# Linear attention in front of two dense layers: numerators and denominators by token from one product, division on the way out of PSUM, quotients transposed back

## Chip, core and metric

One of the eight cores of a Trainium2 chip runs the whole program in one launch. The metric is device time in microseconds (us) of one execution; lower is better. Beside it stands the span, from the first to the last instruction in the profile of one execution.

## What is computed

Attention by random features, for 4 batches, 8 heads, 576 tokens and 64 columns a head, and then two dense layers on its output, which is laid out as 2304 tokens by 512 columns. All inputs are float32.

```python
def phi(x):
    proj = np.einsum('bhsd,md->bhsm', x, omega)
    sq = np.sum(x * x, axis=-1, keepdims=True) / 2.0
    h = proj - sq
    h = h - np.max(h, axis=-1, keepdims=True)
    return np.exp(h) / np.sqrt(m)
q_p, k_p = (phi(q_s), phi(k_s))
kv = np.einsum('bhsm,bhsd->bhmd', k_p, v)
z = np.sum(k_p, axis=2)
num = np.einsum('bhsm,bhmd->bhsd', q_p, kv)
den = np.einsum('bhsm,bhm->bhs', q_p, z)[..., None] + 1e-06
x = num / den                       # then [2304, 512]
x = leaky_relu(x @ w_in, 0.01) @ w_out
h = x @ w_in2
out = (h * clip(h + 3, 0, 6) / 6) @ w_out2
```

There are 128 features (m), so a tile of features of 128 tokens is a square of 128 by 128.

## The kernel before

The program is written as a graph of operations. Each names its engine (or several, with a planned cost for each), what it reads and writes, and a due time; `Graph.run` then plays the program through with those costs and puts every engine's instructions into a fixed order. TensorE's order is therefore decided when the kernel is built, and a matmul that is not ready holds up everything behind it.

**Groups.** The 2304 tokens are cut into five groups of 512, 256, 512, 512 and 512 (`GN`). Group 0 has its attention done first; then the first dense layer (`moe1`) of group 0 runs on TensorE, with the attention of group 1 sprinkled between its matmuls, and so on up to group 4 (the `att` stage, about 47 to 357 us). The second dense layer (`moe2`) of all groups is last, from about 519 us. The dense layers hold each float32 number as two fp32r halves and make a product of three matmuls (lines 497 to 499 in `mm3`, 1067 and 1167).

**Pairs of heads.** The two heads of a pair (e = 0, 1) lie on 64 partitions each. `scores` (L744, with tails of 64 tokens in `K_tail`, L765) multiplies 64 rows of a head by omega, DVE takes the minimum of a row (L709), adds and subtracts squares (L712, POOL L715), and ACT makes the exponentials (L720): the features `h`, one bank for each head, tokens on the partitions.

**K_unit(b, hp)**, 16 of them, 4 in the attention of each of groups 0 to 3 (batch 0 to 3), makes what all queries of a pair of heads need. For batches 0 and 1 (`OLDKV` = 2) `kv` (L791) multiplies features by values, nine matmuls: `v` has a column of ones behind each head's 64, so that column 64 of the result `kvf` (features by 66 columns a head) is z. One copy on ACT (L795) brings it to SBUF, and two matmuls (`rep`, L802) spread z over all partitions as `zr`, which is copied on (L478). For batches 2 and 3 `kvt` (L813) makes the product the other way round, 64 columns of the array for each head, ten matmuls; a copy, a transpose (L820) and a copy give `kvf`, and z is made apart: DVE sums the features over the tiles (L830) or POOL does (L828), POOL adds the tail (L835), and a matmul by ones (L839) sums over the partitions into `zr`.

**Q_first**, four units of group 0, transposes the features (L858), multiplies by all 66 columns of `kvf` (L867), so that numerators and the denominator of a token lie in one row, adds epsilon, takes the reciprocal and multiplies on DVE while reading PSUM (L872, L874, L876), and transposes the quotients back (L885).

**Q_unit** does the queries of groups 1 to 4 in 17 units, each of up to four tiles a head: `f` full tiles of 128 tokens for each of `nh` pairs of heads, and with `half` a tile that holds 64 tokens of both heads. By `f` times `nh` and half tiles: five units have four full tiles, four have three full tiles, four have three full and one half tile, two have two and two, and two have four half tiles alone (17 in all, of which the list `PARTS` gives the tokens). In each, DVE makes the denominators before anything else: for every tile a product of features and `zr` summed along the row (L915, with an instruction that reads the sum), then a reciprocal (L921). POOL or DVE scales the features by it (L926). TensorE transposes the scaled features (L941), they are copied to `tq`, and `num` (L972) multiplies 64 columns of `kvf` by them, for each head, straight into the layout that `moe1` reads (columns on the partitions, tokens along the row).

**PSUM and SBUF.** In the `att` stage attention may hold four of the eight banks at a time (`held` and `share` in `Graph.run`). `keep_warm` (L1364) puts matmuls on zeros where the player of the order expects TensorE to idle in the first stage.

Of the kernel before, what the change touches and what calls it, by code (L numbers as in the profile page):

```python
# [14 lines left out]
ALU = mybir.AluOpType  # L15
# [28 lines left out]
OLDKV = 2  # L44
# [307 lines left out]
def attn_moe_kernel(ctx: ExitStack, tc: tile.TileContext, qT, kT, qn, kn, v1, om2, w1i, w1o, w2i, w2o, out):  # L352
# [23 lines left out]
    def duo(t, later=0):  # L376
# [17 lines left out]
        "junk": many(1, "junk", ([128, 2, 128], BF16), pool=misc),  # L394
# [6 lines left out]
        "zr": many(6, "zr", ([128, 2, 128],), pool=right),  # L401
# [4 lines left out]
        "hh": many(2, "hh", ([128, 128],), pool=right),  # L406
        "ht": many(2, "ht", ([128, 512],), pool=right),
        "tq": many(1, "tq", ([128, 2, 512],), pool=right),
# [56 lines left out]
    ones = sb("ones", [128, 128])  # L465
    zero = sb("zero", [128, 128], F32R)
    slots["den"] = many(3, "den", ([128, 4, 1],), ([128, 4, 1],))
# [256 lines left out]
    def scores(f, half, xsrc, nsrc, due, nh=1):  # L724
# [9 lines left out]
        hs = [Buf("h" if c > 1 else "hh") for c in cols]  # L734
# [36 lines left out]
    kvf, zrep = {}, {}  # L771

    def K_unit(b, hp, due):
        v = Buf("v")
        hs, _ = scores(4, False, kT[b, hp, :, 0:512], kn[b, hp, :, 0:8], due)
        ht = last64[b]
        g.op(dma(lambda: v.tiles[0][:, 0:5 * 132], v1[b, hp], 128 * 5 * 132 * 4), wr=[v], due=due - 7e3)
        zr = zrep[b, hp] = Buf("zr")
        kf = kvf[b, hp] = Buf("kvf")
        p = Ps(g.use)  # L780


        if b < OLDKV:
            def kv():
                todo = [(slice(0, 132), ht.tiles[0][:, hp * 128:hp * 128 + 128], v.tiles[0][:, 4 * 132:5 * 132])]
                for i in range(4):
                    for e in range(2):
                        w = slice(e * 66, e * 66 + 66)
                        todo.append((w, hs[e].tiles[0][:, i * 128:i * 128 + 128], v.tiles[0][:, i * 132 + w.start:i * 132 + w.stop]))
                for n, (w, l, r) in enumerate(todo):  # L790
                    nc.tensor.matmul(p.tiles[0][:, w], lhsT=l, rhs=r, start=n == 0, stop=n == len(todo) - 1, skip_group_check=True)  # L791

            g.op([("pe", 9 * 215.0, kv)], rd=hs + [ht, v], wr=[p], also=[zr, kf], due=due + 3e3)
            kvp = lambda: p.tiles[0][:, 0:132].rearrange("p (h c) -> p h c", h=2)
            g.op([("act", c_act(132, True), lambda: nc.scalar.copy(kf.tiles[0], kvp()))], rd=[p], wr=[kf], due=due + 3e3)  # L795

            flat = lambda: zr.tiles[0].rearrange("p h m -> p (h m)")
            pz = Ps(g.use)

            def rep():  # L800
                for e in range(2):
                    nc.tensor.matmul(pz.tiles[0][:, e * 128:e * 128 + 128], lhsT=kf.tiles[0][:, e, 64:65].to_broadcast([128, 128]),  # L802
                                     rhs=ident, start=True, stop=True)

            g.op([("pe", 360.0, rep)], rd=[(kf, "z")], wr=[pz], due=due + 3.5e3)
            g.op(copy_alts(flat, lambda: pz.tiles[0][:, 0:256], 256, True), rd=[pz], wr=[zr], due=due + 4e3)
            return

        def kvt():
            for i in range(5):  # L810
                for e in range(2):
                    r = ht.tiles[0][:, hp * 128:hp * 128 + 128] if i == 4 else hs[e].tiles[0][:, i * 128:i * 128 + 128]
                    nc.tensor.matmul(p.tiles[0][64 * e:64 * e + 64, 0:128], lhsT=v.tiles[0][:, i * 132 + e * 66:i * 132 + e * 66 + 64], rhs=r,  # L813
                                     start=i == 0, stop=i == 4)

        g.op([("pe", 5 * 224.0, kvt)], rd=hs + [ht, v], wr=[p], also=[zr, kf], due=due + 3e3, mode="N")
        mid = lambda: kf.tiles[0].rearrange("p h c -> p (h c)")[:, 0:128]
        g.op(copy_alts(mid, lambda: p.tiles[0][:, 0:128], 128, True), rd=[p], wr=[kf], due=due + 3e3)
        pt = Ps(g.use)
        g.op([("pe", 112.0, lambda: nc.tensor.transpose(pt.tiles[0][:, 0:128], mid(), ident))], rd=[kf], wr=[pt], due=due + 3e3)  # L820
        g.op(copy_alts(lambda: kf.tiles[0][:, :, 0:64], lambda: pt.tiles[0][:, 0:128].rearrange("p (h c) -> p h c", h=2), 128, True),
             rd=[pt], wr=[kf], due=due + 3.5e3)
        for e in range(2):
            H, Z = lambda e=e, i=0: hs[e].tiles[0][:, i * 128:i * 128 + 128], lambda e=e: zr.tiles[0][:, e]

            def adds(e=e, H=H, Z=Z):
                for i in range(3):
                    nc.gpsimd.tensor_tensor(out=Z(), in0=Z() if i else H(), in1=H(i=i + 1), op=ALU.add)  # L828

            g.op([("dve", c_dve(512), lambda e=e, Z=Z: nc.vector.tensor_reduce(  # L830
                out=Z(), in_=hs[e].tiles[0].rearrange("p (q f) -> p f q", q=4), axis=AX.X, op=ALU.add)),
                ("pool", 3 * c_pool(128), adds)], rd=[hs[e]], wr=[(zr, e)], due=due + 3e3)
            R = lambda e=e: (zr.tiles[0][64 * e:64 * e + 64, e], ht.tiles[0][64 * e:64 * e + 64, hp * 128:hp * 128 + 128])
            g.op([("dve", c_dve(128), lambda R=R: nc.vector.tensor_tensor(out=R()[0], in0=R()[0], in1=R()[1], op=ALU.add), True),
                  ("pool", c_pool(128), lambda R=R: nc.gpsimd.tensor_tensor(out=R()[0], in0=R()[0], in1=R()[1], op=ALU.add))],  # L835
                 rd=[ht], wr=[(zr, e)], due=due + 3e3)
        flat = lambda: zr.tiles[0].rearrange("p h m -> p (h m)")
        pz = Ps(g.use)
        g.op([("pe", 435.0, lambda: nc.tensor.matmul(pz.tiles[0][:, 0:256], lhsT=ones, rhs=flat(), start=True, stop=True))],  # L839
             rd=[zr], wr=[pz], due=due + 3.5e3)  # L840
        g.op(copy_alts(flat, lambda: pz.tiles[0][:, 0:256], 256, True), rd=[pz], wr=[zr], due=due + 4e3)
# [5 lines left out]
    def Q_first(b, hp, due):  # L847
# [14 lines left out]
        for e in range(2):  # L862
            p, den = Ps(g.use), Buf("den")

            def num(e=e, p=p):
# [7 lines left out]
                out=den.tiles[0], in0=view()[:, :, 64:65], scalar1=M * EPS, scalar2=None, op0=ALU.add))], rd=[p], wr=[den], due=due + 6e3)  # L873
            g.op([("dve", 90, lambda den=den: nc.vector.reciprocal(out=den.tiles[1], in_=den.tiles[0]), True)], wr=[den], due=due + 6e3)  # L874
            to = lambda e=e: h.tiles[0].rearrange("p (q e c) -> p q e c", q=4, e=2)[:, :, e]
            g.op([("dve", c_dve(256), lambda view=view, den=den, to=to: nc.vector.tensor_tensor(  # L876
                out=to(), in0=view()[:, :, 0:64], in1=den.tiles[1].to_broadcast([128, 4, 64]), op=ALU.mult))],
# [14 lines left out]
    def Q_unit(grp, b, hps, f, half, s0, col0, o, due):  # L892
# [9 lines left out]
        zr, kf = [zrep[b, hp] for hp in hps], [kvf[b, hp] for hp in hps]  # L902
        tq = Buf("tq")
        wide = N > 256
        ts = [Ps(g.use) for _ in range(2 if wide else 1)]
        todo = []
# [46 lines left out]
        elif f:  # L953
            g.op(copy_alts(lambda: tq.tiles[0][:, :, 0:N], lambda: ts[0].tiles[0].rearrange("p (e n) -> p e n", e=2)[:, :, 0:N], 2 * N, True),
                 rd=[ts[0]], wr=[(tq, 0)], due=due + 5e3)
# [483 lines left out]
```

## Time and profile before

| | us |
|---|---|
| median of three timed runs | 880.21 |
| lowest and highest of them | 878.3, 880.41 |
| the profiled execution's own time | 877.54 |
| its span | 875.7 |
| PE (matmul) busy | 860.1, 98% of the span |
| DVE busy | 651.5, 74% |
| ACT busy | 526.4, 60% |
| POOL busy | 176.5, 20% |

The profile shows one execution. PE is TensorE's matmuls and PEld its loads of weights (the stationary operand), which can lie beside matmuls. A matmul's end is modelled and the next starts before it, so that the time a matmul takes of the stream is read from one start to the next, and busy time counts a run's last tail as well. A float32 (not fp32r) matmul shows as two records, each with its own load of weights; a transpose and an fp32r matmul show as one.

### The profile page before, as it was taken

What the parts mean: (1) busy time and instruction counts of PE and PEld (TensorE: products, weight loads), DVE (VectorE), ACT (ScalarE), POOL (GpSimd) and SP (SyncE); (2) the same over time, 40 slices, a digit from 0 to 9 for tenths busy, and PEclk for the clock granted to TensorE, in tenths of its full rate; (3) what the DMA queues carried; (4) which work ended last, traced back from release to release, by engine and by line L of the source; (5) the groups of instructions that cost most, each with busy time, mean ns of one, the idle gap of its engine ahead of it and who ended that gap; (6) DMA issues with size and microseconds to landing.
All of it is one profiled execution on the core that took longest, in us unless ns stands there. A gap on an engine that the chain in (4) does not pass through costs nothing.

```text
span 875.7 us, 17773 instructions
## 1 busy us (share of the span) xinstructions
PE 860.1 (98%) x6340; PEld 782.0 (89%) x6340; DVE 651.5 (74%) x1641; ACT 526.4 (60%) x1196; POOL 176.5 (20%) x300
## 2 busy tenths in 40 slices
PE   9999999999999999999999999999999999999998
PEld 8878788889777878888888888999999999999998
DVE  6997997977987854566688445787678779877765
ACT  7999987877787755544545345544453455445442
POOL 1132212433334322101110001111102203121200
PEclk9999999999999999999999999999999999999999
DMA  9567656887567720798998448885887685688342
GB/s 332 173 196 244 208 175 200 240 250 232 173 174 223 230 97 12 270 359 335 332 350 330 161 140 281 308 300 170 277 300 247 215 271 164 211 264 258 124 147 71
DMA packets 91496, 198.00 MB, mean 226 GB/s; under 512 B 14736, under 2 KB 40976, under 8 KB 91408
## 3 DMA queue, kind: packets, MB, share of 16 engines
q1 hardware_dynamic: 91408, 196.87, 67.9%
q8 instruction: 50, 0.82, 0.4%
q14 instruction: 38, 0.31, 0.1%
HBM read 150.18 MB, written 46.66 MB: 225 GB/s over the span
## 4 chain that ended last, share of the span: by engine, by line
PE 73%; DVE 9%; ACT 8%; DMA 6%; issue 2%; POOL 1%; SPq 1%; DVEq 0%; ACTq 0%; POOLq 0%
PE bank L1067 18%; PE bank L1167 16%; PE bank L497 11%; PE bank L499 11%; PE bank L498 10%; PE bank L744 2%; DMA late_w<-in 2%; DVE junk L915 1%; ACT h L720 1%; DVE nm L709 1%; DMA out_raw<-wt 1%; DMA in_raw<-wt 1%; DVE wst L537 1%; ACT wt L531 1%; ACT wst L527 1%
## 5 line engine op out<-in xcount | busy, mean ns | idle before, releaser
L1067 PE MATMUL bank<-w,g 128*128 128x256 f32 x720 | 95.9, 275 | 0.5 <-ACT bank L1200 0.3
L478 ACT COPY late_u<-bank 128x256 f32<-128x256 f32 (+1 forms) x103 | 39.9, 388 | 85.6 <-PE bank L1167 76.4
L1067 PEld LDWEIGHTS bank<-w,g 128*128 128x128 f32 x720 | 87.9, 192 | 1.0 <-ACT bank L1200 0.4
L1009 DVE TENSOR_TENSOR g<-bank,g 128x512 fp32r<-128x512 f32 (+1 forms) x80 | 50.6, 633 | 38.9 <-ACT g L478 37.8
L720 ACT ACTIVATE h<-bank,nm 128x128 f32<-128x128 f32 x228 | 64.6, 388 | 17.0 <-POOL nm L715 16.8
L1007 ACT ACTIVATE bank<-bank 128x512 f32<-128x512 f32 (+1 forms) x80 | 44.5, 556 | 49.6 <-PE bank L499 49.5
L497 PE MATMUL bank<-x,w 128*128 128x512 f32 (+1 forms) x180 | 67.1, 373 | 0.6 <-DVE g L1009 0.6
L1167 PE MATMUL bank<-x,late_w 128*128 128x256 f32 x528 | 66.9, 276 | 0.1
L497 PE MATMUL bank<-g,w 128*128 128x512 f32 (+1 forms) x180 | 67.0, 372 | 0.1
L499 PE MATMUL bank<-x,w 128*128 128x512 f32 (+1 forms) x180 | 64.6, 359 | 0.9 <-DVE x L481 0.9
L1167 PE MATMUL bank<-second_w,late_w 128*128 128x256 f32 x474 | 64.7, 275 | 0.8 <-ACT late_u L478 0.5
L499 PE MATMUL bank<-g,w 128*128 128x512 f32 (+1 forms) x180 | 64.6, 359 | 0.5 <-DVE g L1009 0.5
L498 PE MATMUL bank<-x,w 128*128 128x512 f32 (+1 forms) x180 | 64.5, 358 | 0.0
L498 PE MATMUL bank<-g,w 128*128 128x512 f32 (+1 forms) x180 | 64.5, 358 | 0.0
L1167 PEld LDWEIGHTS bank<-x,late_w 128*128 128x128 f32 x528 | 62.8, 192 | 0.5 <-DVE late_xr L485 0.3
L709 DVE TENSOR_REDUCE nm<-bank 128x4 f32<-128x512 f32 (+2 forms) x76 | 47.9, 654 | 20.0 <-PE bank L744 19.7
L1167 PEld LDWEIGHTS bank<-second_w,late_w 128*128 128x128 f32 x474 | 58.9, 192 | 1.4 <-ACT late_u L478 0.7
L478 ACT COPY u<-bank 128x256 f32<-128x256 f32 (+1 forms) x52 | 21.9, 426 | 43.7 <-PE bank L1167 22.2
L715 POOL TENSOR_TENSOR nm<-nm,sq 128x4 f32<-128x4 f32 (+2 forms) x76 | 23.0, 311 | 113.7 <-DVE nm L712 106.8
L915 DVE CUSTOM_DVE_ANT_0 junk<-h,zr 128x128 bf16<-128x128 f32 (+1 forms) x128 | 44.1, 381 | 1.3 <-ACT h L720 0.6
L497 PE MATMUL bank<-x,second_w 128*128 128x512 f32 (+1 forms) x120 | 44.1, 368 | 0.8 <-ACT tq L478 0.8
L926 POOL TENSOR_TENSOR h<-h,den 128x512 f32<-128x512 f32 (+2 forms) x32 | 34.0, 1065 | 53.4 <-DVE den L921 42.3
(377 smaller groups left out, 2395.9 us busy)
## 6 DMA issues: line engine op xcount, KB each, us to landing
late_w<-in SPq DMA_DIRECT2D x85, 512.0 KB, 4.5
in<-late_w SPq DMA_DIRECT2D x32, 512.0 KB, 4.4
late_w<-in SPq DMA_DIRECT2D x39, 256.0 KB, 4.8
third_w<-in SPq DMA_DIRECT2D x19, 512.0 KB, 4.8
wst<-w2i SPq DMA_DIRECT2D x16, 512.0 KB, 4.2
wst<-w2o SPq DMA_DIRECT2D x16, 512.0 KB, 4.6
x_t<-late_w SPq DMA_DIRECT2D x12, 512.0 KB, 5.5
v<-v SPq DMA_DIRECT2D x14, 330.0 KB, 4.8
```

The lines of the kernel that those rows point to most:

```text
L478: return [("act", c_act(n, psum), lambda: nc.scalar.copy(dst(), src())), dve if psum else dve + (True,)]
L497: nc.tensor.matmul(o, lhsT=ah, rhs=bh, start=start, stop=False)
L498: nc.tensor.matmul(o, lhsT=al, rhs=bh, start=False, stop=False)
L499: nc.tensor.matmul(o, lhsT=ah, rhs=bl, start=False, stop=stop)
L709: g.op([("dve", c_dve(c * 128), lambda raw=raw, n_=n_: nc.vector.tensor_reduce(out=n_()[:, :, 0], in_=raw(), axis=AX.X, op=ALU.min))], rd= ...
L720: nc.scalar.activation(h.tiles[0][:, q * 128:q * 128 + 128], raw()[:, q], AF.Exp, bias=nm.tiles[0][:, q], scale=-1.0)
L915: nc.vector.tensor_tensor_reduce(out=jk.tiles[0][r, q % 2], in0=h.tiles[0][r, q * 128:q * 128 + 128], in1=zr[k].tiles[0][r, e], scale=1.0, ...
L926: eng.tensor_tensor(out=x, in0=x, in1=den.tiles[1][:, 0:c].to_broadcast([128, c, 128]), op=ALU.mult)
L1007: g.op([("act", c_act(n, True), lambda: nc.scalar.activation(P(), P(), AF.Prelu, alpha=0.01))], wr=[p], due=d)
L1009: g.op([("dve", c_dve(n), lambda: nc.vector.tensor_tensor(out=G1(), in0=P(), in1=G0().bitcast(F32), op=ALU.subtract))], rd=[p, (gg, 0)], w ...
L1067: nc.tensor.matmul(acc[bank].tiles[0][:, half * 256:half * 256 + 256], lhsT=src.tiles[x][:, q * 128:q * 128 + 128], rhs=woven(w[k].tiles[y ...
L1167: nc.tensor.matmul(R[r](), lhsT=w[x], rhs=m[y], start=start and k == n == 0, stop=k == 1 and n == 2, skip_group_check=True)
```

## The change

`Q_unit` of groups 1 to 4 is rebuilt after the pattern of `Q_first`. The scaling ahead of the transposes, the denominators on DVE (L915, L921, L926) and `num` (L972) go. The unscaled features are transposed by bank and copied to `tq`. A new function `quotient` multiplies `tq` by 66 columns of `kvf` for each full tile, or by all 132 for a half tile (whose rows hold 64 tokens of each head), adds epsilon and takes the reciprocal, and divides while reading PSUM into `qt`; for half tiles the reciprocals are first multiplied by a mask `own`, which keeps a row's own head. `back` transposes `qt` to where `num` wrote, and a half tile goes through a matmul with `fold` (two identities of 64 rows, one above the other) instead.

In `K_unit` every batch uses `kv`, without `rep`: `zr`, `kvt`, the transpose, the sums on DVE and POOL and the matmul by ones go. Its planned cost is 220 + 8 times 112 ns where it was 9 times 215; `num`'s in `quotient` is 112 ns a matmul. Buffers: `zr`, `hh`, `ones` and `junk` go, a second `tq`, one `qt`, `fold` and `own` come, `den` has 8 columns. The start gains one DVE addition (`fold`) and three small memsets.

```diff
         "kvf": many(6, "kvf", ([128, 2, 66],), pool=right),
-        "zr": many(6, "zr", ([128, 2, 128],), pool=right),
...
-        "tq": many(1, "tq", ([128, 2, 512],), pool=right),
+        "tq": many(2, "tq", ([128, 2, 512],), pool=right),
+        "qt": many(1, "qt", ([128, 512],), pool=right),
...
-        if b < OLDKV:
-            def kv():
...
-            g.op([("pe", 9 * 215.0, kv)], rd=hs + [ht, v], wr=[p], also=[zr, kf], due=due + 3e3)
...
-            g.op([("pe", 360.0, rep)], rd=[(kf, "z")], wr=[pz], due=due + 3.5e3)
...
-        g.op([("pe", 5 * 224.0, kvt)], rd=hs + [ht, v], wr=[p], also=[zr, kf], due=due + 3e3, mode="N")
...
-        g.op([("pe", 435.0, lambda: nc.tensor.matmul(pz.tiles[0][:, 0:256], lhsT=ones, rhs=flat(), start=True, stop=True))],
...
+        g.op([("pe", 220.0 + 8 * 112.0, kv)], rd=hs + [ht, v], wr=[p], also=[kf], due=due + 3e3)
+        kvp = lambda: p.tiles[0][:, 0:132].rearrange("p (h c) -> p h c", h=2)
+        g.op(copy_alts(lambda: kf.tiles[0], kvp, 132, True), rd=[p], wr=[kf], due=due + 3e3)
...
-                        nc.vector.tensor_tensor_reduce(out=jk.tiles[0][r, q % 2], in0=h.tiles[0][r, q * 128:q * 128 + 128],
-                                                       in1=zr[k].tiles[0][r, e], scale=1.0, scalar=M * EPS, op0=ALU.mult,
-                                                       op1=ALU.add, accum_out=den.tiles[0][r, q])
...
+            def num():
+                at = 0
+                for e, q, m in todo:
+                    w = 132 if m[1] is None else 66
+                    r = kf[m[0]].tiles[0].rearrange("p h c -> p (h c)") if m[1] is None else kf[m[0]].tiles[0][:, m[1]]
+                    nc.tensor.matmul(p.tiles[0][:, at:at + w], lhsT=tq.tiles[0][:, e, q * 128:q * 128 + 128], rhs=r, start=True, stop=True)
+                    at += w
...
+            g.op([("dve", 75, lambda: nc.vector.tensor_scalar(out=dd(0), in0=V()[:, :, :, 64:65], scalar1=M * EPS, scalar2=None, op0=ALU.add))],
+                 rd=[p], wr=[den], due=due + 6e3)
...
+            g.op([("dve", c_dve(tiles * 64), lambda: nc.vector.tensor_tensor(
+                out=to(), in0=V()[:, :, :, 0:64], in1=dd(1).to_broadcast([128, dd(1).shape[1], dd(1).shape[2], 64]), op=ALU.mult))],
+                rd=[p, den], wr=[(qt, sub)], due=due + 6e3)
...
-                    nc.tensor.matmul(p.tiles[0][64 * e:64 * e + 64, k * n:k * n + n], lhsT=kf[k].tiles[0][:, e, 0:64],
-                                     rhs=tq.tiles[0][:, e, k * n:k * n + n], start=True, stop=True)
...
+                for i in range(f):
+                    c = (k * f + i) * 128
+                    nc.tensor.transpose(p.tiles[0][:, k * n + i * 128:k * n + i * 128 + 128], qt.tiles[0][:, c:c + 128], ident)
+                if half:
+                    c = (T + k) * 128
+                    nc.tensor.matmul(p.tiles[0][:, k * n + F:k * n + n], lhsT=qt.tiles[0][:, c:c + 128], rhs=fold, start=True, stop=True)
```

In the changed kernel the lines move: `mm3` is 495 to 497, `scores` 742, `kv` 787, the transposes of the features 860, `num` 875, the division 881 to 889, `back` 921 and 924, `keep_warm` 1318. Counted over the whole program, TensorE has 72 `kv` matmuls more (144 for 72), 96 `num` matmuls of 66 columns and 16 of 132, 48 transposes and 16 folds in `back`, and 44 matmuls on zeros for 36.

The first place is the batch-2 K_unit on PE. Before: ten matmuls of 64 array columns (`h`, `ht` features, `v` values), and behind other work the transpose of `kvf` and the matmul by `ones`.

```order
L499 MATMUL bank_177<-x_104,w_95 128x256
L813 MATMUL bank_182<-h_0_149,v_0_144 64x128
L813 MATMUL bank_182<-h_0_145,v_0_144 64x128
...
L813 MATMUL bank_182<-ht_0_152,v_0_144 64x128 x2
L497 MATMUL bank_180<-g_105,w_94 128x256
...
L820 MATMUL bank_181<-ident,kvf_0_130 128x128
...
L839 MATMUL bank_178<-zr_0_136,ones 128x256
```

The changed kernel, the same unit:

```order
L921 MATMUL bank_176<-ident,qt_0_147 128x128 x3
L787 MATMUL bank_170<-v_0_137,ht_0_143 128x132
L787 MATMUL bank_170<-v_0_137,h_0_139 128x66
L787 MATMUL bank_170<-v_0_137,h_0_140 128x66
...
L787 MATMUL bank_170<-v_0_137,h_0_140 128x66
L495 MATMUL bank_175<-g_106,w_90 128x256
```

Nine matmuls of 128 array columns stand there in one run, and nothing of the unit comes later on PE.

The second place is a query unit of group 4 (one pair of heads, four full tiles) on PE. Before: both banks of features (`h`) are transposed together, and `num` follows 15 dense matmuls later.

```order
L941 MATMUL bank_177<-ident,h_0_145 128x128 x4
L941 MATMUL bank_176<-ident,h_0_147 128x128 x4
L497 MATMUL bank_180<-g_106,second_w_5_0_1039 128x512
...
L499 MATMUL bank_178<-x_102,second_w_8_0_1042 128x512
L972 MATMUL bank_182<-tq_0_154,kvf_0_130 64x512 x2
L497 MATMUL bank_178<-x_103,second_w_8_0_1042 128x512
```

The changed kernel:

```order
L860 MATMUL bank_176<-ident,h_0_142 128x128 x4
...
L860 MATMUL bank_173<-ident,h_0_139 128x128 x4
L875 MATMUL bank_169<-kvf_0_129,tq_0_146 128x66 x4
L495 MATMUL bank_170<-x_103,second_w_6_0_1012 128x512
...
L875 MATMUL bank_176<-kvf_0_129,tq_0_146 128x66 x4
L495 MATMUL bank_171<-g_106,second_w_5_0_1011 128x512
...
L497 MATMUL bank_173<-x_102,second_w_8_0_1014 128x512
L921 MATMUL bank_169<-ident,qt_0_147 128x128 x4
L495 MATMUL bank_173<-x_103,second_w_8_0_1014 128x512
```

Two wide matmuls have become eight narrow ones in two runs, 9 dense matmuls apart, and four transposes come 15 dense matmuls after the second.

## Rows read from the trace of the kernel before

**Rows 1.** The page: span, and busy time by engine.

```profile
span 875.7 us, 17773 instructions
...
PE 860.1 (98%) x6340; PEld 782.0 (89%) x6340; DVE 651.5 (74%) x1641; ACT 526.4 (60%) x1196; POOL 176.5 (20%) x300
...
PEclk9999999999999999999999999999999999999999
```

**Rows 2.** The page: the chain that ended last, by engine.

```profile
PE 73%; DVE 9%; ACT 8%; DMA 6%; issue 2%; POOL 1%; SPq 1%; DVEq 0%; ACTq 0%; POOLq 0%
```

**Rows 3.** Waits of PE: who waited for whom, us in total, times, longest.

```profile
PE bank L499 <- DVE g L1009: 1.3, 2, 0.8
PE bank L1364 <- POOL zero L1355: 1.1, 1, 1.1
PE bank L499 <- DVE x L481: 0.9, 1, 0.9
PE bank L885 <- DVE u L876: 0.8, 1, 0.8
...
PE bank L497 <- DVE g L1009: 0.6, 1, 0.6
```

**Rows 4.** Timeline of PE: start, us, instruction; a kv run between dense matmuls.

```profile
115.03 0.38 PE L499 MATMUL bank<-x,second_w 128*128 128x512 f32 x1
115.25 0.39 PE L791 MATMUL bank<-v,ht 128*128 128x132 f32 x2
115.47 1.90 PE L791 MATMUL bank<-v,h 128*128 128x66 f32 x16
...
117.47 0.38 PE L498 MATMUL bank<-x,second_w 128*128 128x512 f32 x1
```

**Rows 5.** Timeline of PE: a query unit's num, then transposes, between dense matmuls.

```profile
316.55 0.38 PE L499 MATMUL bank<-g,w 128*128 128x512 f32 x1
316.86 1.08 PE L972 MATMUL bank<-tq,kvf 128*64 128x512 f32 x4
...
318.19 0.38 PE L498 MATMUL bank<-x,second_w 128*128 128x512 f32 x1
318.40 0.38 PE L499 MATMUL bank<-x,second_w 128*128 128x512 f32 x1
318.62 1.04 PE L941 MATMUL bank<-ident,h 128*128 128x128 f32 x8
...
319.71 0.38 PE L498 MATMUL bank<-x,second_w 128*128 128x512 f32 x1
```

**Rows 6.** Timeline of PE: a kvt run of batch 2 between dense matmuls.

```profile
187.48 0.28 PE L498 MATMUL bank<-x,w 128*128 128x256 f32 x1
187.60 0.28 PE L499 MATMUL bank<-x,w 128*128 128x256 f32 x1
187.80 1.09 PE L813 MATMUL bank<-h,v 128*64 128x128 f32 x16
...
189.26 0.28 PE L498 MATMUL bank<-g,w 128*128 128x256 f32 x1
```

**Rows 7.** Groups by line on PE: busy us, mean ns; idle before, releasers.

```profile
L972 PE MATMUL bank<-tq,kvf 128*64 128x64 f32 (+5 forms) x112 | 15.9, 395 | 0.0
L1364 PE MATMUL bank<-zero 128*128 128x384 f32 x36 | 10.1, 432 | 1.1 <-POOL zero L1355 1.1
L802 PE MATMUL bank<-ident,kvf 128*128 128x128 f32 x32 | 5.3, 288 | 0.7 <-ACT kvf L795 0.7
L839 PE MATMUL bank<-zr,ones 128*128 128x256 f32 x16 | 5.2, 408 | 1.1 <-ACT h L720 0.6 <-POOL zr L835 0.5
```

**Rows 8.** Groups by line on DVE and POOL, same columns.

```profile
L915 DVE CUSTOM_DVE_ANT_0 junk<-h,zr 128x128 bf16<-128x128 f32 (+1 forms) x128 | 44.1, 381 | 1.3 <-ACT h L720 0.6
L876 DVE TENSOR_TENSOR u<-bank,den 128x256 f32<-128x256 f32 x8 | 3.3, 416 | 0.0
L874 DVE RECIPROCAL den<-den 128x4 f32<-128x4 f32 x8 | 1.4, 169 | 0.0
L872 DVE TENSOR_SCALAR den<-bank 128x4 f32<-128x4 f32 x8 | 1.2, 155 | 0.3 <-ACT zr L478 0.2
L926 POOL TENSOR_TENSOR h<-h,den 128x512 f32<-128x512 f32 (+2 forms) x32 | 34.0, 1065 | 53.4 <-DVE den L921 42.3 <-DVE nm L712 3.3 <-ACT wst L527 2.4
```

More of the change, by code (lines that the diff above doesn't have):

```diff
@@ L464, in attn_moe_kernel @@
     wn = sb("wn", [128, 128])
[L465 removed]
     zero = sb("zero", [128, 128], F32R)
[L467 removed]
+    slots["den"] = many(3, "den", ([128, 8, 1],), ([128, 8, 1],))
+    fold = sb("fold", [128, 64])
+    own = sb("own", [128, 2, 1])
     three = sb("three", [128, 8], pool=misc)[:, 0:1]
@@ L733, in scores @@
         ps = [Ps(g.use) for _ in cols]
-        hs = [Buf("h" if c > 1 else "hh") for c in cols]
+        hs = [Buf("h") for c in cols]
         def mm():
@@ L823, in K_unit @@
[L823 to L836, printed above, removed]
@@ L956, in Q_unit, with tr @@
-        if half:
-            from_ = lambda: ts[1 if wide else 0].tiles[0][:, nh * F:nh * F + nh * 128].rearrange("p (h e n) -> p e h n", h=nh, e=2)
-            g.op(copy_alts(lambda: T()[:, :, :, F:n], from_, nh * 128, True), rd=[ts[1 if wide else 0]], wr=[(tq, 2)], due=due + 5e3)
+        kf, tq, qt = [kvf[b, hp] for hp in hps], Buf("tq"), Buf("qt")
+        T = nh * f
+        for bank, (h, c) in enumerate(zip(hs, cols)):
+            ts = Ps(g.use)
+            def tr(h=h, ts=ts, c=c):
+                for q in range(c):
+                    x = slice(q * 128, q * 128 + 128)
+                    nc.tensor.transpose(ts.tiles[0][:, x], h.tiles[0][:, x], ident)
+            g.op([("pe", c * 109.0, tr)], rd=[h], wr=[ts], also=[tq], due=due + 5e3)
+            g.op(copy_alts(lambda bank=bank, c=c: tq.tiles[0][:, bank, 0:c * 128], lambda ts=ts, c=c: ts.tiles[0][:, 0:c * 128], c * 128, True),
+                 rd=[ts], wr=[(tq, bank)], due=due + 5e3)
@@ new lines, in Q_unit @@
+        full = lambda: qt.tiles[0][:, 0:T * 128].rearrange("p (t e c) -> p e t c", e=2, c=64)
+        for es in ([0, 1],) if T <= 3 else ([0], [1]):
+            if T:
+                w = len(es) * T * 66
+                todo = [(e, (k * (f + half) if e == 0 else k * f) + i, (k, e)) for e in es for k in range(nh) for i in range(f)]
+                quotient(todo, [(tq, e) for e in es], len(es) * T, len(todo) * 112.0,
+                         lambda t, w=w, es=es: t[:, 0:w].rearrange("p (e t c) -> p e t c", e=len(es), c=66),
+                         lambda es=es: full()[:, es[0]:es[-1] + 1], False, es[0])
@@ L959, in Q_unit @@
+        for k0 in range(0, nh if half else 0, 2):
+            ks = range(k0, min(nh, k0 + 2))
+            c = T * 128 + k0 * 128
+            quotient([(0, k * (f + half) + f, (k, None)) for k in ks], [(tq, 0)], 2 * len(ks), len(ks) * 224.0,
+                     lambda t, m=len(ks): t[:, 0:m * 132].rearrange("p (k e c) -> p k e c", k=m, c=66),
+                     lambda c=c, m=len(ks): qt.tiles[0][:, c:c + m * 128].rearrange("p (k e c) -> p k e c", k=m, c=64), True, 2 + k0)
         away = grp == NG - 1
@@ L1356, in attn_moe_kernel @@
         make_identity(nc, ident)
+        nc.vector.tensor_tensor(out=fold, in0=ident[:, 0:64], in1=ident[:, 64:128], op=ALU.add)
+        nc.vector.memset(own, 0.0)
+        nc.vector.memset(own[0:64, 0], 1.0)
+        nc.vector.memset(own[64:128, 1], 1.0)
         nc.vector.tensor_scalar(out=wn, in0=wn, scalar1=-scale, scalar2=None, op0=ALU.mult)
```

115 lines of the change are left out of this document (26 added, 89 removed).

## The prediction

> **What bounds the kernel now.** I read the page's busy times first: PE is busy for 860.1 of a span of 875.7 us, DVE for 651.5, POOL for 176.5, and the clock row is at 9 in every slice, so TensorE runs at its upper level of 2.4 GHz throughout [rows 1]. The chain that ended last is PE for 73% of the span [rows 2]. What PE does not fill is 875.7 - 860.1 = 15.6 us, and that is the most that any relief of another engine can bring. The waits of PE show where part of it lies: dense matmuls that wait for DVE's low half of their operands (L499 and L497 for g L1009, 1.3 and 0.6 us, and L499 for x L481, 0.9), a transpose in Q_first that waits 0.8 us for its quotient (L885), and 1.1 us at the start [rows 3]. The groups by line add 0.7 us ahead of L802 and 1.1 ahead of L839 [rows 7]. So the question is how much TensorE time the change adds, for nearly all of it lies on the path.
>
> **The price of a matmul on PE.** It is read from starts, not from durations. Dense matmuls of 512 columns start 0.216 us apart (318.19 to 318.40, the last digit rounded) [rows 5], those of 256 columns 0.112 (187.48 to 187.60) [rows 6]. A run of something else between two of them costs the time from the last dense start before to the second dense start behind it, less two dense steps; the second, because the first one behind a run is itself held up.
>
> - kv, nine float32 matmuls and thus 18 records: 117.47 - 115.03 = 2.44, less 0.43, is 2.01 us, or 0.112 a record and 0.224 a matmul [rows 4]. Eight of the nine have 66 columns, so this is the price of a matmul of 66 columns.
> - num for 512 tokens: 318.19 - 316.55 = 1.64, less 0.43, is 1.21 us, where its busy time is 1.08; the run pays 0.12 or so beyond its busy time, on the way into and out of half the array's columns [rows 5].
> - eight transposes: 319.71 - 318.40 = 1.31, less 0.43, is 0.88, or 0.110 each [rows 5].
> - kvt: 189.26 - 187.60 = 1.66, less two steps of 0.112, is 1.44 us [rows 6].
>
> The program plans a 66-column matmul at 112 ns, half of what the row shows. The Trainium skill says under "FP8 and Floating Point Precision", section TensorE Precision Notes, that a true float32 product takes four passes through the array. By it alone, 66 columns four times are 264 columns, at 2.4 GHz an estimated 110 ns, which is the planned price and would make this change cheap. The row does not agree: kv takes 0.224, the pace of its two loads of weights rather than of its columns, and the sum below goes by the row.
>
> **What goes from PE.** num in 17 units: 15.9 us busy [rows 7] and 17 times 0.12, 17.9. kvt in 8 units, 8 times 1.44 = 11.5. Behind each a transpose at 0.110, 0.9, and the matmul by ones: its two records are busy for 5.2 / 8 = 0.65 us, of which a part overlaps what follows [rows 7]; two steps of a 512-column record, 0.43, are my value, so 3.5 in all (it could be 5.2). The spreading of z in the 8 other units is four records at 0.112, 0.45, so 3.6 (busy 5.3 at most [rows 7]). Together 37.4 us, up to 40.8 with the two upper ends.
>
> **What comes to PE.** Eight more kv runs at 2.01, 16.1. In quotient 96 matmuls of 66 columns and 16 of 132, all at 0.224 (the kv run holds one of 132 and is no dearer), 25.1. In back 48 transposes at 0.110, 5.3. The 16 folds have 64 columns, a form that the trace doesn't show: at least a transpose, 0.110, at most a kv matmul, 0.224; they are float32 products with 128 rows of weights, as kv is, so 0.224, 3.6 (1.8 at the least). Together 50.1. The transposes of the features stay the same number. The eight more matmuls on zeros cost nothing if PE would have idled there and 10.1 / 36 = 0.28 each at most, 2.2 us [rows 7]; I take half, 1.1. PE gains 50.1 + 1.1 - 37.4 = 13.8 us of work, between 7.5 (folds cheap, zeros free, the removed ones at their busy time) and 15.
>
> **What leaves the other engines.** DVE loses the 44.1 us of L915, POOL the 34.0 us of L926 [rows 8]. DVE gains 30 quotients of 0.155 + 0.169 + 0.416 = 0.74 us, 22 us, priced by the same three instructions of Q_first [rows 8]. This is worth nothing in itself, because both lie beside PE; it is worth what PE waited for them. The waits ahead of L802 and L839 go with these instructions, 0.7 + 1.1 = 1.8 us [rows 7]. The three dense waits for DVE, 1.3 + 0.9 + 0.6 = 2.8 [rows 3], should go too, because DVE no longer has runs of L915 of 381 ns apiece between PE and the low half that PE waits for. That is 4.6 us back. It can be nothing, or the whole 15.6 less the 1.1 of the start, 14.5.
>
> **The waits that the change adds.** A quotient waits for its num, and back waits for both quotients with all dense matmuls of the next rows queued behind it. In the query unit of group 4 shown above, 15 dense matmuls at 0.216, 3.2 us, stand between the second num and back, while DVE needs 0.74 and the signals, which leaves room for other work ahead of it in DVE's queue. The cover is long enough there. num waits for the copy of tq, which has 9 dense matmuls of cover and the other head's run for either head. A second tq lets the next unit begin before the last is through. At the start, fold and three memsets go onto DVE while the first scores wait for their input, and cost nothing. SP gets no further transfers. I price new waits at zero.
>
> **The sum.** 13.8 - 4.6 = 9.2 us longer. The profiled execution had 877.54 us and its span with 1.8 us around it; so 886.7 for such an execution. The median of the runs is 880.21, 2.7 above the profiled one, and the forecast is for a median: 880.2 + 9.2 gives 889.4, rounded to **890 us**. About 0.3% is what a measurement of this kernel can tell from no change, 2.6 us to either side of 880.2.
>
> **Rivals.**
>
> - *The division becomes a wait on PE.* Unlike the scaling by POOL, the quotient stands between two matmul steps of the same unit. If back, in all 17 units, waited as L885 did in Q_first, 0.8 us [rows 3], that were 13.6 us, and no relief elsewhere: 880.2 + 13.8 + 13.6 = 908. For it: Q_first has this very pattern and does wait. Against: there PE has little else to put between, here it has 3.2 us of dense matmuls. It decides once DVE takes over 3 us from num to the last product. Half of it gives 898. Chance 0.13.
> - *All waits go.* DVE and POOL are so much lighter that PE hardly idles any more: 880.2 + 13.8 - 14.5 = 879.5, within 0.3%. For it: DVE at 74% is the engine behind most of the waits that rows name. Against: those waits add up to a third of the 15.6, and the rest also lies in the second layer and at the start, where nothing changes. It needs more than 11 us of the 15.6. Chance 0.08.
> - *The planned price holds, and the kernel becomes faster.* If a 66-column matmul in quotient and kv ran at the pace of its columns, at 0.112, the 64 new ones in kv and 96 in quotient would be 160 times 0.112 = 17.9 us cheaper: 13.8 - 17.9 - 4.6 = -8.7, or 871.5 us. The skill's rule of four passes, named above, speaks for it. Against it stand the rows of kv in this very form [rows 4], and nothing in the new product lets two loads of weights overlap. The point is 0.14 us a matmul: below it the added work is less than the waits won. Chance 0.05. That the change would not do what it says isn't among the rivals, since the order of instructions shows the new matmuls.
>
> **How the numbers follow.** The forecast with its own bounds (work 7.5 to 15, relief 0 to 7) has 0.74 and holds 881 to 896. The range reaches into half of the first rival and to the upper part of the second: **882 to 901**. Faster by over 0.3% is the third rival and a little of the second's tail: 0.06. Within 0.3%, up to 882.8: the second rival and the lower edge of the forecast, 0.10. Slower: 0.84.
>
> **What would show it.** In the profile after: 288 records of kv where there were 144, and 224 of num in quotient, both starting 0.112 us apart; back's transposes 0.110 apart; PE busy near 874 us; DVE busy at most 651.5 - 44.1 + 22 = 629 us and POOL at most 143. The second layer should take as long as before, and the whole loss should lie ahead of it. I am wrong if num runs at under 0.14 us a matmul, if PE's idle time is over 20 us with back or num as the one that waits, or if it falls below 5.

## The result, and the profile after

The changed kernel is slower, by about as much as forecast. Its median is 888.94 us (four runs, 887.38 to 889.85), that of the kernel before beside it 879.25 (876.5 to 880.41); the ratio is 1.0113, with an interval of 1.0083 to 1.0143. The forecast was 890 us, 882 to 901.

| | before | after |
|---|---|---|
| median of the runs, us | 879.25 | 888.94 |
| profiled execution: own time, us | 877.54 | 889.85 |
| its span, us | 875.7 | 888.1 |
| PE busy, us | 860.1 | 873.1 |
| PE idle (span less busy), us | 15.6 | 15.0 |
| DVE / ACT / POOL busy, us | 651.5 / 526.4 / 176.5 | 613.6 / 515.6 / 130.6 |

The two profiled executions lie 12.3 us apart, the medians 9.7. In the later comparisons the kernel before has medians of 876.8 to 877.3, and the change run again gave 888.5 against 876.95, a ratio of 1.0132 (1.0113 to 1.0151). One more run of that comparison, at a granted clock of 0.85 and 993.73 us, is left out of these two numbers. So the loss is 10 to 12 us.

The page of the changed kernel: span, busy times, the clock row, and the chain that ended last, by engine.

```profile
span 888.1 us, 17662 instructions
...
PE 873.1 (98%) x6468; PEld 811.2 (91%) x6468; DVE 613.6 (69%) x1440; ACT 515.6 (58%) x1159; POOL 130.6 (15%) x243
...
PEclk9999999999999999999999999999999999999999
...
PE 85%; ACT 5%; DMA 3%; DVE 2%; issue 1%; POOL 0%; DVEq 0%; ACTq 0%
```

Beside [rows 1] PE has 13.0 us more work in the span, DVE 38 and POOL 46 us less. PE's share of the chain went from 73% [rows 2] to 85%: the end is set by TensorE alone even more than before.

The groups on PE that the change made or enlarged (line, engine, operation, operands, count | busy us, mean ns | idle time just before and who ended it):

```profile
L875 PE MATMUL bank<-kvf,tq 128*128 128x66 f32 (+1 forms) x224 | 29.5, 273 | 0.6 <-DVE g L960 0.6
...
L787 PE MATMUL bank<-v,h 128*128 128x66 f32 x192 | 22.8, 272 | 0.0
...
L1318 PE MATMUL bank<-zero 128*128 128x384 f32 x44 | 12.5, 422 | 1.0 <-POOL zero L1305 1.0
...
L921 PE MATMUL bank<-ident,qt 128*128 128x128 f32 x48 | 8.3, 279 | 0.0
...
L924 PE MATMUL bank<-fold,qt 128*128 128x64 f32 x32 | 4.6, 258 | 0.0
```

The 224 records of `num` are the 112 matmuls of the diff, two records each, and the 16 folds are 32 records. The price stands in the timeline of PE (start, us, instruction), where a run of `num` lies between dense matmuls:

```profile
327.34 0.38 PE L497 MATMUL bank<-x,second_w 128*128 128x512 f32 x1
327.56 1.00 PE L875 MATMUL bank<-kvf,tq 128*128 128x66 f32 x8
...
328.67 0.38 PE L496 MATMUL bank<-x,second_w 128*128 128x512 f32 x1
```

From the last dense start before the run to the second behind it are 328.67 - 327.34 = 1.33 us, less two dense steps, 0.43, is 0.90 for four matmuls: 0.224 each, as `kv` before [rows 4]. For the same 512 tokens of one head the old `num` had cost half of 1.21 [rows 5], 0.6. The Trainium skill, "TensorE: Matmul & The Clock Gate", section LDWEIGHTS (loading the stationary operand), puts a load of P columns at P / 1.2 ns, for 128 columns an estimate of 107 ns. The trace agrees within 5%: each of the two records of a matmul takes 0.112 us, though only 66 columns pass. Four folds in a run, a form that the kernel before did not have, lie between dense starts at 65.89 and 67.21 us: 1.32, less 0.43, is 0.89, or 0.22 each, as priced.

The waits of PE (who waited for whom, us in total, times, longest):

```profile
PE bank L1118 <- DMA late_w<-in: 2.7, 4, 1.5
PE bank L835 <- DVE u L826: 1.3, 1, 1.3
PE bank L495 <- DVE qt L889: 1.2, 1, 1.2
PE bank L1318 <- POOL zero L1305: 1.0, 1, 1.0
PE bank L817 <- DVE tq L475: 0.9, 1, 0.9
PE bank L875 <- DVE g L960: 0.6, 1, 0.6
PE bank L742 <- DVE qt L889: 0.5, 1, 0.5
```

The dense waits for `g` and `x` of [rows 3] are gone. In their place the quotient `qt` is waited for twice, 1.7 us together. Those two and the 0.6 of L875, 2.3 us, are all the waits of PE that its rows show between 47 and 519 us. The kernel before has 6.5 us of them between 47 and 509, for beside the rows of [rows 3] and [rows 7] it has these and smaller ones:

```profile
PE bank L497 <- ACT tq L478: 0.8, 1, 0.8
...
PE bank L941 <- ACT h L720: 0.7, 1, 0.7
```

Where the time went is read from windows: the first stage, attention, and what follows, cut at the same work in both kernels within 1.3 us (the first dense matmul starts at 46.92 us before and at 48.20 after). The columns are the stretch, its length, busy us of PE, PEld, DVE, ACT and POOL, the granted clock, the DMA share and GB/s. Before:

```profile
0.00:47.00 47.00, 44.11 (x397) 40.31 (x397) 37.61 (x99) 40.21 (x115) 6.75 (x27) 1.00 0.74 253
47.00:509.00 462.00, 455.25 (x2817) 385.28 (x2818) 345.21 (x852) 315.78 (x730) 107.18 (x160) 1.00 0.69 226
509.00:875.70 366.70, 360.75 (x3129) 356.46 (x3127) 268.66 (x692) 170.43 (x352) 62.55 (x114) 1.00 0.67 222
```

After:

```profile
0.00:47.00 47.00, 42.92 (x372) 38.91 (x372) 35.70 (x99) 37.84 (x108) 7.72 (x26) 1.00 0.71 238
47.00:519.00 472.00, 469.69 (x2973) 416.10 (x2972) 309.67 (x651) 307.38 (x700) 60.29 (x103) 1.00 0.67 223
519.00:888.10 369.10, 360.50 (x3128) 356.20 (x3126) 268.21 (x692) 170.37 (x352) 62.54 (x114) 1.00 0.67 221
```

In the middle stretch PE works 14.4 us more, of which 1.2 belong to the first stage, that ends later, and idles 462.0 - 455.3 = 6.7 us before, 2.3 after: 4.4 us of waits go. In the first stage PE idles 1.2 us more, and behind attention 8.6 - 6.0 = 2.6 more, where the work is the same.

### The profile page after: what moved, and what is told of

The parts are those of the page before. It is cut to its first block, busy times and chain, and to the rows that moved or that the text cites. A ratio compares the mean times of both kernels' runs of the same rounds, so it can differ in the third digit from the quotient of the medians.

```text
span 888.1 us, 17662 instructions
## 1 busy us (share of the span) xinstructions
PE 873.1 (98%) x6468; PEld 811.2 (91%) x6468; DVE 613.6 (69%) x1440; ACT 515.6 (58%) x1159; POOL 130.6 (15%) x243
## 4 chain that ended last, share of the span: by engine, by line
PE 85%; ACT 5%; DMA 3%; DVE 2%; issue 1%; POOL 0%; DVEq 0%; ACTq 0%
PE bank L1018 18%; PE bank L1118 16%; PE bank L495 14%; PE bank L497 13%; PE bank L496 13%; PE bank L742 3%; PE bank L787 3%; PE bank L875 3%; DMA late_w<-in 2%; PE bank L860 1%; PE bank L921 1%; DMA third_w<-in 1%; ACT stage_wt L529 1%; ACT wt L529 1%; ACT stage_wst L525 1%
## 5 line engine op out<-in xcount | busy, mean ns | idle before, releaser
L476 ACT CAST g<-bank 128x512 fp32r<-128x512 f32 (+1 forms) x77 | 42.9, 557 | 1.5
L479 DVE TENSOR_TENSOR g<-xr,g 128x384 fp32r<-128x384 f32 (+1 forms) x53 | 33.6, 635 | 14.1 <-ACT g L476 13.7
```

The lines of the kernel that those rows point to most:

```text
L476: return [("act", c_act(n, psum), lambda: nc.scalar.copy(dst(), src())), dve if psum else dve + (True,)]
L479: return [("dve", c_dve(n), lambda: nc.vector.tensor_tensor(out=dst(), in0=src(), in1=hi().bitcast(F32), op=ALU.subtract), True), ("pool", ...
```

## The experiments

Ratios are to the kernel before, run beside each on the same chip.

**kv everywhere, the query part as before.** The part of the change in `K_unit` that swaps the product, made in the kernel before. The change goes further: it also drops the spreading of z (`rep`), which this kernel has in all 16 units.

```diff
-OLDKV = 2
+OLDKV = 4
```

> The kernel before with the key units of batches 2 and 3 made by the nine kv matmuls and the two that spread z (OLDKV = 4); queries as before. Theory (every float32 matmul costs 0.224 us, two records at 0.112, whatever its columns up to 132): 8 units change from 1.44 + 0.11 + 0.44 = 1.99 us on PE to 2.01 + 0.45 = 2.46, which is +3.8 us; the waits ahead of the matmul by ones (1.1 us) can go, so +2.5 to +4 against before, 0.3 to 0.45%. Rival (66 columns cost 0.112): kv would take 1.1 us and the kernel would be 8 times 0.4 = 3 us faster.

It took 878.62 us, ratio 1.0010 (0.9996 to 1.0025), about 1 us more than before, with an interval that holds no loss at all. PE has 2.7 us more work than in [rows 1], DVE 8 and POOL 24 less:

```profile
PE 862.8 (98%) x6332; PEld 789.0 (90%) x6332; DVE 643.4 (73%) x1636; ACT 520.5 (59%) x1185; POOL 152.8 (17%) x260
```

The added runs cost 2.01 us each, as priced, and the rival of a gain falls. The loss is smaller than the 2.5 to 4 expected. In the profiled executions the last dense matmul of the first layer starts at 534.30 us instead of 534.05, so up to there nearly all of the added work came back: PE idles 3.8 us in attention instead of 6.7. That this is because DVE and POOL lost the sums of z is likely but not shown. So some 9 to 11 us of the loss belong to the rest of the change; that is a difference of two runs, and the query part was not run alone.

**kv in fewer places.** The opposite step, the old product for one batch more:

```diff
-OLDKV = 2
+OLDKV = 1
```

> The kernel before with the key units of batch 1 made by kvt too (OLDKV = 1). On PE 4 units change from 2.01 + 0.45 = 2.46 to 1.44 + 0.11 + 0.44 = 1.99 us, which is 1.9 us less. Theory (PE's work decides): 1 to 2 us under before, ratio 0.998 to 0.999. Rival (the sums on DVE and POOL, 2 a unit of about 1 us, come in the stretch from 50 to 130 us where DVE is fullest, and PE waits for them): no gain, or 1 to 3 us more.

It took 877.71 us, ratio 1.0007 (0.9991 to 1.0023): no gain. PE's busy time fell by 5.0 us (to 855.1) where 1.9 of work were priced (what the rest is was not traced), the span of the profiled execution by 0.4 (875.3). The other 4.6 turned into waiting, most of it for the sums of z, as the rival has it; the first of its waits of PE was 0.5 us before [rows 7]:

```profile
PE bank L839 <- POOL zr L835: 4.5, 3, 2.3
```

The choice between the two products for the features, one way or the other, is within what can be measured here.

**No division.** Taken from the kernel before: sums, reciprocals and scaling of the query units, as a bound on what relief of DVE and POOL can bring.

```diff
-            den, jk = Buf("den"), Buf("junk")
...
-            g.op([("dve", (c + split_) * 213.0, dn, True)], rd=[h] + zr, wr=[den, jk], due=due + 4e3)
...
-            g.op([("dve", c_dve(w), lambda sc=sc: sc(nc.vector), True), ("pool", 150 + w * 1.85, lambda sc=sc: sc(nc.gpsimd))],
-                 rd=[den], wr=[h], due=due + 4e3)
```

> The kernel before without denominators, reciprocals and scaling in the query units of groups 1 to 4 (their output is left undivided); all matmuls stay. It shows what DVE's and POOL's relief alone is worth. Theory: the dense matmuls' waits for DVE, 2.8 us, mostly go: 2 to 4 us under before, 875 to 877. Rivals: nothing (879), because PE's waits only change place; or nearly all of PE's 14.5 us of idle time, 865 to 868.

It took 874.89 us, ratio 0.9973 (0.9958 to 0.9987): 2.4 us less, though DVE lost 40 us and POOL 38.

```profile
PE 858.1 (98%) x6340; PEld 781.1 (89%) x6340; DVE 611.8 (70%) x1371; ACT 515.4 (59%) x1177; POOL 138.7 (16%) x269
```

The first of its waits of PE is one that was 0.7 us before [rows 7]:

```profile
PE bank L802 <- ACT kvf L795: 3.1, 4, 2.0
```

The dense waits for `g` and `x` are gone, as in the change, but the spreading of z (`rep`, L802), which the change removes, waits longer instead. Nearly 80 us less on two engines beside TensorE buy 2.4 us.

**Truer planned costs.** The changed kernel, with the costs of `kv`, `num` and the folds planned as the rows show them:

```diff
-        g.op([("pe", 220.0 + 8 * 112.0, kv)], rd=hs + [ht, v], wr=[p], also=[kf], due=due + 3e3)
+        g.op([("pe", 9 * 224.0, kv)], rd=hs + [ht, v], wr=[p], also=[kf], due=due + 3e3)
...
-                quotient(todo, [(tq, e) for e in es], len(es) * T, len(todo) * 112.0,
+                quotient(todo, [(tq, e) for e in es], len(es) * T, len(todo) * 224.0,
...
-        g.op([("pe", (T + nh * half) * 111.0, back)], rd=[qt], wr=[p], also=[x for x, _ in outs], due=due + 7e3)
+        g.op([("pe", T * 111.0 + nh * half * 224.0, back)], rd=[qt], wr=[p], also=[x for x, _ in outs], due=due + 7e3)
```

> The changed kernel with the planned costs set to what the trace shows (kv 9 times 224 ns, num 224 a matmul, fold 224). The work is the same but for 8 matmuls on zeros fewer. Theory (the loss is work on PE, not order): 0 to 2.2 us less than the changed kernel, so 886.5 to 889, or 1.008 to 1.011 times before. Rival (the loss comes from an order that was made for wrong costs): most of the 9.7 us come back, 880 to 882.

It missed: 891.97 us, ratio 1.0166 (1.0144 to 1.0187), some 3 us slower than the change itself. There are 36 matmuls on zeros instead of 44, and the first dense matmul starts at 45.7 us instead of 48.2; but by 370 us the kernel is 3 us behind the change. Among its waits of PE are

```profile
PE bank L860 <- ACT h L718: 2.1, 1, 2.1
PE bank L495 <- DVE qt L889: 1.6, 1, 1.6
...
PE bank L875 <- ACT xr L476: 1.0, 1, 1.0
```

where the change has 1.2 for the second, 0.6 for L875 and no row for the first. So the planned price that is half the measured one isn't what makes the change slow. Why a truer plan gives an order with more waits stays open.

**The change again.** The changed kernel without an edit, for the comparison with the last one.

> The changed kernel itself, beside the kernel before on one chip, to place the kernel with true costs against it. Theory: 888 to 890, ratio 1.010 to 1.013, so that the kernel with true costs (1.0166) is slower than it. Rival (that run was on a slower chip): 891 to 893, ratio near 1.016, and the order would have made no difference.

888.5 us, ratio 1.0132 (1.0113 to 1.0151), so the rival of a slower chip falls. The interval of the truer costs lies mostly above it.

**num twice.** Each matmul of `num` in the changed kernel issued twice, to measure its price on the path:

```diff
-                    nc.tensor.matmul(p.tiles[0][:, at:at + w], lhsT=tq.tiles[0][:, e, q * 128:q * 128 + 128], rhs=r, start=True, stop=True)
+                    for _ in range(2):
+                        nc.tensor.matmul(p.tiles[0][:, at:at + w], lhsT=tq.tiles[0][:, e, q * 128:q * 128 + 128], rhs=r, start=True, stop=True)
```

> The changed kernel with each of the 112 num matmuls of groups 1 to 4 issued twice, same result, same planned costs and so the same order. Theory (0.224 us each, all on the path): 112 times 0.224 = 25.1 us more than the changed kernel, 913 to 914. Rival (0.112 each, or half of them in time that PE would have idled): 12.5 us more, 901.

909.82 us, ratio 1.0371 (1.0354 to 1.0388), 21.3 more than the change beside it. The timeline of PE gives the price of eight matmuls in a run:

```profile
345.47 0.38 PE L497 MATMUL bank<-x,second_w 128*128 128x512 f32 x1
345.68 1.90 PE L876 MATMUL bank<-kvf,tq 128*128 128x66 f32 x16
...
347.69 0.38 PE L496 MATMUL bank<-x,second_w 128*128 128x512 f32 x1
```

347.69 - 345.47 = 2.22, less 0.43, is 1.79, or 0.224 each: the price holds to the third digit, and the rival at half of it falls. The time grew by 21.3 of the 25.1 us of work. In the window from 47 us to the end of attention PE idles only 0.5 us:

```profile
47.00:540.00 493.00, 492.51 (x3190) 439.60 (x3189) 308.69 (x650) 306.83 (x699) 61.67 (x103) 1.00 0.64 214
```

The change has 2.3 there, so 1.8 us of the difference are waits that the added work covers. Another 1.5 lie in the second layer, which took that much less in this profiled execution at the same work; the rest, under 1 us, stays open.

**One record for num.** The question was what makes the matmul cost 0.224. In the changed kernel `tq` and `kvf` become fp32r, a type whose product is one record instead of two (the values are rounded to it):

```diff
-        "kvf": many(6, "kvf", ([128, 2, 66],), pool=right),
+        "kvf": many(6, "kvf", ([128, 2, 66], F32R), pool=right),
...
-        "tq": many(2, "tq", ([128, 2, 512],), pool=right),
+        "tq": many(2, "tq", ([128, 2, 512], F32R), pool=right),
```

> The changed kernel with tq and kvf held as fp32r, so that each num matmul of queries is one record instead of two; the products are rounded to fp32r, which the reference's are not. Theory (num is paid by records at 0.112, each with its own load of weights): 112 matmuls of groups 1 to 4 and 32 of group 0 lose a record each, 12.5 + 3.6 us, so about 873 us, 0.7% under before; the records of num stay 0.112 apart although they then have 66 columns only. Rival (paid by columns and passes): a record of 66 columns in one pass would start 0.03 to 0.06 us after the one before, and the time fall by 20 us or more, to under 869.

879.72 us, ratio 1.0023 (1.0006 to 1.0040). That is 9.2 us less than the change, where 16 were expected. The price fell as the theory says (timeline of PE, a run of four matmuls):

```profile
322.74 0.38 PE L497 MATMUL bank<-x,second_w 128*128 128x512 f32 x1
322.96 0.53 PE L875 MATMUL bank<-kvf,tq 128*128 128x66 f32 x4
...
323.62 0.38 PE L496 MATMUL bank<-x,second_w 128*128 128x512 f32 x1
```

323.62 - 322.74 = 0.88, less 0.43, is 0.45 for four, half of 0.90 at the same 66 columns. So the price goes by records, each with its load, and not by these columns. A row of before points the same way: the 20 records of `kvt`, with half the columns of weights but 128 passing, cost 1.44 us [rows 6], 0.072 each. What fell short was the rest. Behind 46 us, the attention work between dense matmuls takes 102.5 us instead of 113.1, that is 10.6 of the 12.5 us that 112 records fewer would give there; but in the first stage nothing was won. The first dense matmul starts at 48.4 us against 48.2, Q_first's transpose waits 2.5 us for its quotient, and TensorE's clock fell:

```profile
PE bank L835 <- DVE u L826: 2.5, 1, 2.5
```

The clock fell in attention too, about 48 to 51 us and 112 to 116. There dense matmuls of 512 columns start 0.42 or 0.43 us apart instead of 0.216 (timeline of PE, then a window with the columns of the windows above):

```profile
49.44 0.63 PE L497 MATMUL bank<-x,w 128*128 128x512 f32 x1
49.86 0.63 PE L495 MATMUL bank<-x,w 128*128 128x512 f32 x1
...
112.00:116.00 4.00, 4.00 (x13) 3.19 (x12) 3.11 (x10) 2.42 (x7) 0.51 (x3) 0.59 0.26 59
```

Over the two stretches the dense matmuls lose about 2.8 us in this way, and of the 10.6 won, 7.0 are left at the last dense matmul of the first layer (536.80 us for 543.84); some 0.5 of the difference was not traced.

**One record for kv too.** Features and a copy of the values become fp32r as well, and groups 1 to 4 have one `tq` again, for room:

```diff
-        "h": many(5, "h", ([128, 512],), pool=right),
+        "h": many(5, "h", ([128, 512], F32R), pool=right),
...
+        g.op(copy_alts(lambda: vr.tiles[0][:, 0:5 * 132], lambda: v.tiles[0][:, 0:5 * 132], 660), rd=[v], wr=[vr], due=due)
...
-                    nc.tensor.transpose(ts.tiles[0][:, x], h.tiles[0][:, x], ident)
+                    nc.tensor.transpose(ts.tiles[0][:, x].bitcast(F32R), h.tiles[0][:, x], identr)
```

> The kernel with num in one record, and also the kv matmuls in one record: features and a copy of the values (made by ACT or DVE, 660 columns a unit) held as fp32r, one tq for groups 1 to 4 instead of two for room; products rounded to fp32r. Theory (0.112 a record): 12 kv units in groups 1 to 3 lose 9 records, 12.1 us; the 4 in group 0 gain little, since there the chain through ACT and DVE sets the time (the kernel with num in one record gained nothing before 48 us); so 12 us under that kernel's 879.7: 866 to 870, about 1% under before. Rival (PE then waits for the copies and for the one tq): 875 or more.

869.28 us, ratio 0.9906 (0.9890 to 0.9922): faster than both kernels, as expected, with 851.2 us of PE work.

**Two orders of that kernel.** One plans Q_first's `num` at its new price (450 for 900 ns), the other also plans more matmuls on zeros:

```diff
-    FILL = 0.5
+    FILL = 1.0
```

> The kernel with num and kv in one record, with the planned cost of num in the first stage at its new price (450 for 900), which puts 59 matmuls on zeros into that stage instead of 46. There the granted clock had fallen to half for 17 us of the first 48. Theory (less TensorE work in the first stage made the clock fall; the stage is bound by the chain through ACT and DVE and by the half clock): fewer half-clock microseconds, first dense matmul at 48 instead of 49.2, 868 to 869 against 869.3. Rival (the zeros only stand in the way): 870 to 871.

> The same with twice the filling (108 matmuls on zeros). Theory: no half clock from 10 us on, first dense matmul at 46.5 to 48, 867 to 869. Rival (the zeros delay the attention's own matmuls, about 49 more at 0.16 us, 8 us at most): 870 or more.

The first took 869.62 us, 0.9917 (0.9890 to 0.9944): no gain that can be measured. The second, with 108 zeros where the changed kernel has 44, took 867.79 us, 0.9888 (0.9865 to 0.9911). It is the best version found, 1.1% under the kernel before and 2.4% under the change; its lead over the other two versions with `kv` in one record lies within the intervals.

## Why the prediction was right, and where its sum was off

**The price of a float32 matmul of 66 columns** held. 0.224 us was read from a kv run before [rows 4], and the new runs cost 0.224; doubling them added 0.224 each, and halving their records halved them. This step decided the sign. By the Trainium skill's four passes ("FP8 and Floating Point Precision", TensorE Precision Notes) the estimate was 110 ns, and the runs disagree at 66 columns. A wider product is another matter. The matmul by ones in the kernel before, with 256 columns, takes 203.50 - 202.85 = 0.65, less two dense steps of 0.112, 0.43 us, which is also the value taken for it in the prediction:

```profile
202.85 0.28 PE L499 MATMUL bank<-x,second_w 128*128 128x256 f32 x1
202.96 0.60 PE L839 MATMUL bank<-zr,ones 128*128 128x256 f32 x2
...
203.50 0.28 PE L498 MATMUL bank<-g,w 128*128 128x256 f32 x1
```

Four passes of 256 columns, by that section of the Trainium skill, would be an estimate of 427 ns, and there the trace agrees. At 66 and at 132 columns (115.25 to 115.47 [rows 4]) the price is 0.22, at 256 it is 0.43: for the narrow products it no longer falls with the columns. One step in the rivals was mis-worked, without effect: the 9.2 us of the sum over 160 matmuls are 0.058 each, so the change would have broken even at 0.167 us a matmul, not at 0.14.

**The work on PE** was forecast to grow by 13.8 us; PE is busy for 13.0 more, 873.1 where "near 874" was expected.

**The relief** of 4.6 us and **new waits at zero** came out right as a sum, and that is partly luck: idle time in attention fell by 4.4. The waits named for the relief did go, but so did the others there, 6.5 us in all; and 2.3 us of new ones came. Each term was off by about 2, and the two errors cancel. The size of the relief rested on rows of single waits, and the run without the division, where the dense waits for `g` and `x` went too and the whole time fell by only 2.4, shows that such a sum can be given back elsewhere. How light DVE would get was mis-sized: I counted the 44.1 us of L915 and 22 for the quotients, and gave 629 as the most; it is 613.6. I left out what goes with L915, as the groups of DVE before show (the reads of its accumulator, the sums of z):

```profile
L915 DVE DVE_READ_ACCUMULATOR2_ANT den<- 128x1 f32 (+1 forms) x128 | 10.1, 79 | 0.0
...
L830 DVE TENSOR_REDUCE zr<-h 128x128 f32<-128x512 f32 x8 | 8.5, 1059 | 0.0
```

Of the new waits two are for `qt`, 1.7 us together, against 13.6 in the rival where all 17 units wait; that rival falls.

**Outside attention** the sum had nothing, and the profile shows 3.8 us. In the first stage PE idles 1.2 us more; L835 waits 1.3 us for `u` instead of 0.8 for its counterpart [rows 3], and L817 0.9 for `tq`. That belongs to the kernel: the first dense matmul starts at 48.2 us here and at 48.4 with `num` twice, but at 46.8 to 47.3 in the kernel before and its three variants. With the truer planned costs it is at 45.7, so it hangs on the planned order; what in that order costs the time was not tried.

"The second layer should take as long as before": PE's work there is the same (360.75 and 360.50), but it idles 2.6 us more. Waits for the weights `late_w` by DMA are 2.7 us in the rows after, and before they are

```profile
PE bank L1167 <- DMA late_w<-in: 0.5, 2, 0.3
```

Whether this belongs to the change is open. From the last dense matmul of the first layer to the end the two executions take 341.65 and 344.26 us, the nine other kernels traced 340.3 to 342.9, kinds of the changed kernel among them, and each has one execution in its trace. The one of the change, at 889.85 us, is the longest of its four runs.

By profiled executions the loss is thus 12.3 us and not 9.2: 13.0 of work, 4.4 back in attention, 3.8 lost again at both ends, which is 12.4 of span. Up to the last dense matmul of the first layer it is 9.8 (543.84 for 534.05). That the median of 888.94 lies so close to 890 is partly luck too: the sum of 9.2 is short of a loss of 10 to 12, and the 880.21 that it was added to lies 1 to 3 us above the later medians of the kernel before.

**The other rivals.** "All waits go" needed PE to idle under 5 us; it idles 15.0. "The planned price holds" is excluded by the price itself.

## What to carry to other kernels

Price small float32 matmuls by what a run of them takes between two known starts, and count their records: here a matmul of 66 columns with 128 columns of weights costs two records, each with its load, 0.224 us, and the product with one record half of that. When TensorE is busy for 98% of the span, work added to it is mostly paid: 21 us of 25 with `num` twice, 12 of span for 13 of busy time in the change. But a small step can vanish in waits, as the swap of the product for the features did both ways, while 80 us taken from DVE and POOL bring 2 or 3. And judge a stall removed by what waits next: much of the work that was saved by the old product in one batch more turned into waiting, and the relief without division into a wait elsewhere.

## What was not expected of the hardware

TensorE's clock fell in the first stage once its matmuls lost records, and with one record for `num` in attention too (0.59 of full speed from 112 to 116 us, see there). The granted clock of two stretches, same columns as the windows above; first the changed kernel:

```profile
20.00:35.00 15.00, 14.85 (x137) 13.25 (x136) 13.34 (x38) 13.51 (x42) 4.21 (x11) 1.00 0.57 183
35.00:50.00 15.00, 12.53 (x101) 11.24 (x100) 13.50 (x34) 13.04 (x33) 2.71 (x3) 1.00 0.61 193
```

With one record for `num`:

```profile
35.00:50.00 15.00, 12.23 (x79) 10.81 (x80) 12.20 (x33) 12.08 (x29) 2.58 (x3) 0.82 0.60 195
```

With one record for `kv` too:

```profile
20.00:35.00 15.00, 14.60 (x114) 13.56 (x112) 12.03 (x29) 12.98 (x40) 0.94 (x6) 0.66 0.56 175
35.00:50.00 15.00, 13.93 (x81) 11.89 (x80) 13.55 (x37) 14.87 (x38) 4.13 (x7) 0.77 0.60 180
```

And that kernel with 108 zeros:

```profile
20.00:35.00 15.00, 15.00 (x145) 13.87 (x144) 14.04 (x37) 14.85 (x49) 2.38 (x9) 1.00 0.57 175
35.00:50.00 15.00, 14.92 (x107) 13.72 (x106) 13.95 (x33) 14.94 (x33) 6.41 (x7) 1.00 0.73 235
```

In the third kernel the clock stood at 1.2 GHz for 17 of the first 48 us. The busy time doesn't tell this ahead: 12.53 of 15 us went with the full clock in one kernel, 14.60 with 0.66 in another, for at the lower clock the same matmuls stay busy longer. More matmuls on zeros gave the full clock back for the whole first stage; in attention this kernel still has 3 us at 0.57, from 111 to 114. The Trainium skill, "TensorE: Matmul & The Clock Gate", section What's actually happening, has the array throttled by default and released by activity, with which this agrees. What it was worth is small: from 869.62 to 867.79 us between the last two kernels, within their intervals, since the first dense matmul starts at 48.7 and 47.5 us.
